# Attention and SiLU MLP on one core: the value products of 39 of 512 key groups as three float16 products of parts

## The chip, the cores and the metric

One core of one Trainium2 chip runs the whole program. The metric is the device time of one execution in microseconds (us); the number to compare is the median of several runs. A difference of under about 0.2% cannot be told from no change here: the three runs of the kernel before lie within 0.66 us of each other.

## The reference

One pre-LayerNorm transformer layer on 2048 tokens of width 512, in float32:

```python
h  = x + softmax((q @ k.T) * 16**-0.5) @ v @ wo      # q, k, v = layernorm(x) @ wqkv; 32 heads of 16
h2 = h + silu(layernorm(h) @ w1) @ w2                # inner width 1792
```

## The kernel before, in words

**Precision.** Most products are of float16 parts: a float32 matrix is split into a high part and the low rest (`low`: rest = matrix - high part), and a product is three products: high by high, low by high, high by low. So it is for the projections, the scores and the MLP. One product stays in float32: the value products, in which the weights of the softmax (`pt`) meet the values (`va`). `PE` here is TensorE, `DVE` VectorE, `ACT` ScalarE, `POOL` GpSimd, `SP` the engine that issues the DMAs.

**Items, groups, steps.** The attention works on 32 items: an item is 4 heads and a block of 512 queries, and items 8b to 8b+7 make block b. An item goes through 16 groups of 128 keys. For a group and a head, `scores` (L495) makes one matrix product of 64 rows into one PSUM bank of kind `st`: 128 keys by 512 queries, where rows 48 and 49 of the operand hold minus the maximum, so that it is subtracted in the product. `weigh` (L504) then has ACT take the exponential of the bank into a tile `pt` of 128 x 512 float32. The scale of that activation comes from a register of ACT (`qk_f`, loaded at L624), and its bias is left at the default. `values` (L893) does the four value products of a group: the 17 columns of `va` of each head (16 and one of ones, which sums the weights) are the weights of TensorE, 128 x 17, in four column groups side by side, and the `pt` of each head streams through; all sum into the bank `pv` over the 16 groups. `finish_item` (L911) copies `pv` out (`pvs`; by DVE in block 0, by ACT later), and sends the sums through DRAM so that POOL can invert them (`invert`, L980), and the result is multiplied by the inverses.

The main loop (L1461) makes one step per group g: maxima for later items, the scores and exponentials of the step, at the end the value products of group g-2 (`LAG = 2`, L1548). `maximum` (L291) finds the maxima that later items need: a product of 48 rows (high parts alone) into one of three banks of kind `sm`, and a `TENSOR_REDUCE` by DVE. Products of 48 or 64 rows take one half of the array's rows, and two of them, in the two halves, run side by side.

**Kinds of steps.** In a *plain* step (block 0's 8 items, and a few steps around the output stages) there are four scores, three maxima, the value products and nothing else; `st` has four banks. Block b's output projection and normalization (`output`, L1291) is put into steps of item 8(b+1). Then, from group 16(8b+9)+4 on, 112 groups carry block b's MLP *beside* them (L485): 56 groups of *first products* (w1), then 56 of *second products* (w2). `beside_products` (L1243) orders such a step: on one half of the array's rows four scores and maxima take turns, on the other six half products of the MLP. One of the four `st` banks then serves the MLP's sum, so that the scores of such a step have three. In a step beside, the scores are of one row half: heads 0 and 2 of groups g and g+1 in an even step, heads 1 and 3 of groups g-1 and g in an odd one. A chain of first products takes 4 steps and ends with `end_first` (L1161): ACT copies the sum out (`g`), two steps later ACT takes a tanh (`t`), and POOL makes the SiLU and its two parts in four instructions (`bend`, L1165). A chain of second products takes 14 steps and ends with `end_second` (L1175): ACT copies the sum (`g`), POOL adds it.

**Order.** Each engine runs its instructions in the order in which the code emits them (`keep_in_program_order`), and waits on semaphores; nothing is reordered by a scheduler. A step is emitted as a whole, so ACT's and POOL's orders follow the steps too.

**Buffers.** `pt` tiles are in two rings, of 6 and 8 (`pt_tile`, L492). Keys and queries of an item lie in a ring of 5 slots (`ks`, `qs`), loaded four items ahead (L256, L261). `zp` has two buffers each for `g` and for the tag `oh` (`t`, `o_t`).

Of the kernel before, what the change touches and what calls it, by code (L numbers as in the profile page):

```python
# [10 lines left out]
F32 = mybir.dt.float32  # L11
F32R = mybir.dt.float32r
F16 = mybir.dt.float16
# [26 lines left out]

BOUND = 23.0
# [8 lines left out]
PTS = 6, 8  # L50

RING = 5

# [14 lines left out]
MORE = (5, 4, 4, 4), (5, 4, 4, 3), (5, 4, 4, 3)  # L68
# [23 lines left out]
def attention_mlp_kernel(ctx: ExitStack, tc: tile.TileContext, x, wqkv, wo, w1, w2, out):  # L92
# [98 lines left out]
    expo = expos[:, :1]  # L191
    minus = const.tile([P, 16], F32, name="minus")
    nc.gpsimd.memset(minus, -1.0)
    ones = const.tile([P, P], F32, name="ones")
    nc.gpsimd.memset(ones, 1.0)
    powers = const.tile([P, 4], F32, name="powers")
    both_s, both_w = powers[:, :2], powers[:, 2:]
    qk_s, qk_w, v_w = (powers[:, n:n + 1] for n in (0, 2, 3))
    qk_e, qk_0, v_f = (const.tile([P, 1], F32, name=name) for name in ("qk_e", "qk_0", "v_f"))
# [3 lines left out]
    w1_s, w2_s, wo_s, o_s = (sigma[:, n:n + 1] for n in range(4))  # L203
# [48 lines left out]

    def rows_of_head(t, h):
        return t[h * DH:(h + 1) * DH].rearrange("d s n -> (d s) n")

    def load_k(i, k, lo=0, n=S):  # L256
        a, j = HEADS[k]
        h = 4 * (i % 8) + 2 * a + j
        dma(ks[i % RING][64 * j:64 * j + 48, a, lo:lo + n], rows_of_head(kd, h)[:, lo:lo + n])

    def load_q(i, k):  # L261
        a, j = HEADS[k]
        h = 4 * (i % 8) + 2 * a + j
        lo = i // 8 * 512
        dma(qs[i % RING][64 * j:64 * j + 48, a, :], rows_of_head(qd, h)[:, lo:lo + 512])
# [25 lines left out]
    def maximum(i, kb, qt, a, j, n):  # L291

        piece = piece_of(i, a)
        width = 1 if i == LAST else 2
        if piece not in mx:
            mx[piece] = small.tile([P, 64], F32, name="mx", bufs=RING + 1)[:, :32 * width].rearrange(
                "p (j a q k) -> p j a q k", j=2, a=width, k=4)
            left[piece] = 32 * width
        heads = (0, 1) if j is None else (j,)
        for m, h in enumerate(heads):  # L300
            mm(space[:, n + m, :], qs[i % RING][64 * h:64 * h + 48, a, qt * P:qt * P + P],
               ks[i % RING][64 * h:64 * h + 48, a, kb * 512:kb * 512 + 512], start=True, stop=True)
# [47 lines left out]
    def place_far(piece):  # L350

        i, a = piece
        n = 16 if a is None else 8
        mt = small.tile([P, P], F16, name="mt", bufs=1)
        pin(nc.sync.dma_start(mt, wide.pop(piece), transpose=True))
        split.pop(piece)

        def out():
            for j in range(2):
                rows = qs[i % RING][64 * j + 48:64 * j + 50, slice(None) if a is None else slice(a, a + 1)]  # L360
                dma(rows.rearrange("r a n -> r (a n)").rearrange("r (a b) -> r a b", b=P), mt[n * j:n * j + n, :])
            placed.add(piece)

        if at["attention"]:
            soon(1, out)
        else:
            out()

    def place_max(piece):

        i, a = piece
        ns = split.pop(piece)
        n = ns.shape[1]
        ps = bank("sm", F16)
        tr(ps[:n, :P], ns, ident_h)
        mt = small.tile([32, P], F16, name="mn", bufs=1)[:n]
        dve("tensor_copy", mt, ps[:n, :P])

        def out():
            for j in range(2):  # L380
                dst = qs[i % RING][64 * j + 48:64 * j + 50, slice(None) if a is None else slice(a, a + 1)]
# [110 lines left out]
    def pt_tile(name, second, dtype=F32):  # L492
        return bp.tile([P, 512], dtype, tag=f"pt{second}", name=name, bufs=PTS[second])

    def scores(g, k, kind="st"):  # L495

        i = g // KC
        a, j, c = head(g, k)
        assert piece_of(i, a) in placed
        ps = bank(kind)  # L500
        mm(ps, ks[i % RING][64 * j:64 * j + 64, a, c * P:(c + 1) * P], qs[i % RING][64 * j:64 * j + 64, a, :],
           start=True, stop=True)
# [40 lines left out]
    rest_sq = const.tile([P, sum(PIECES)], F32, name="rest_sq")  # L543
# [25 lines left out]
    def set_factors():  # L569
# [4 lines left out]
        for to, a, f in ((h_f, inverse[:, :1], 1 / LN), (g_s, w1_s, 1 / 32.0), (g_half, w1_s, 1 / 64.0),  # L574
                         (out_f, inverse[:, :1], 32.0), (o_minus, o_s, -1.0), (o_twice, o_s, 2.0)):
            pool("tensor_scalar", to, a, f, None, op0=ALU.mult)
        pool("tensor_tensor", out_f, out_f, inverse[:, 1:2], ALU.mult)
# [28 lines left out]
    def measure(meanwhile):  # L606
# [13 lines left out]
        dve("reciprocal", v_f, v_w)  # L620
        pool("tensor_scalar", v_f, v_f, 1 / LN, None, op0=ALU.mult)
# [43 lines left out]
    def project_v(b, t):  # L665
# [4 lines left out]
        act("mul", va[:, 4 * b + t, :, 0:DH], ps.rearrange("p (h d) -> p h d", d=DH), v_f)  # L670
# [100 lines left out]
    for b in range(NB):  # L771
# [7 lines left out]
        for n, (kind, k) in enumerate(units + vs if b else units):  # L779
# [160 lines left out]
    def finish_part():  # L940
        pvs = bp.tile([P, 512], F32, name="pvs", bufs=1)
        dve("tensor_copy", pvs, pv)
        o_t = zp.tile([P, 4, P], F32, name="o_t", tag="oh")
# [5 lines left out]
    def divide_part(part, pvs, o_t, kind="st"):  # L949
# [4 lines left out]
        both = gp.tile([P, 4, 2, DH + 1], F32, name="both", bufs=1)  # L954
# [4 lines left out]
        dve("tensor_scalar", rc, rc, o_s, None, op0=ALU.mult)  # L959
# [105 lines left out]
    def load_rows(b, t):  # L1065
        n = 4 * b + t
        if b < NB - 1:
            hx[t] = raw_tile()
        else:
            hx[t] = ks[(LAST + 1) % RING].rearrange("p a n -> p (a n)").bitcast(F32)[:, t * D:(t + 1) * D]  # L1070
# [20 lines left out]
    def gate(ps, engine="dve"):  # L1091
        g, parts = zp.tile([P, 512], F32, name="g"), parts_of(pt_tile("gh", 1))
# [68 lines left out]
    def end_first(f, ps):  # L1161
# [3 lines left out]
        def bend():  # L1165
            t = zp.tile([P, 512], F32, name="t", tag="oh")
# [263 lines left out]
    def maxima(g):  # L1430

        i, c = divmod(g, KC)
        ready = at["ready"] = min(ITEMS, i + RING - (0 if c == KC - 1 else 1)) * 64
# [27 lines left out]
    for g in range(groups):  # L1461
# [11 lines left out]
        if i + RING - 1 < ITEMS and 6 <= c < 14:  # L1473
            (load_k if c % 2 else load_q)(i + RING - 1, c // 2 - 3)
# [30 lines left out]
        if g == 1:  # L1505
            dve("memset", pv, 0.0)
        at["group"] = g
# [76 lines left out]
```

## Time and profile before

| | |
|---|---|
| median of 3 runs | 1549.03 us (1548.48 to 1549.14) |
| the profiled execution | 1548.43 us |
| its span, first to last instruction | 1546.6 us |
| outside the span | 1.8 us |
| PE, DVE, ACT, POOL busy | 99%, 88%, 80%, 37% of the span |
| steps of attention | 180.4 to about 1452 us of the span |

The profile is of one execution. A row that groups instructions has engine, operation, out<-in, shapes and count, then busy time, mean duration of one, and the idle time before them with what ended it. A row of the timeline has the start, how long it took, engine, line, operation and count; equal instructions that follow each other are one row, so the start of a row and the count tell the spacing. `PEld` are weight loads. Ends of matmuls are modelled, so starts are used where a spacing matters. A row of windows has the stretch, its length, then for each engine busy time and count in it.

### The profile page before, as it was taken

What the parts mean: (1) busy time and instruction counts of PE and PEld (TensorE: products, weight loads), DVE (VectorE), ACT (ScalarE), POOL (GpSimd) and SP (SyncE); (2) the same over time, 40 slices, a digit from 0 to 9 for tenths busy, and PEclk for the clock granted to TensorE, in tenths of its full rate; (3) what the DMA queues carried; (4) which work ended last, traced back from release to release, by engine and by line L of the source; (5) the groups of instructions that cost most, each with busy time, mean ns of one, the idle gap of its engine ahead of it and who ended that gap; (6) DMA issues with size and microseconds to landing.
All of it is one profiled execution on the core that took longest, in us unless ns stands there. A gap on an engine that the chain in (4) does not pass through costs nothing.

```text
span 1546.6 us, 30865 instructions
## 1 busy us (share of the span) xinstructions
PE 1536.2 (99%) x11408; PEld 495.2 (32%) x11408; DVE 1365.3 (88%) x2168; ACT 1238.1 (80%) x2410; POOL 576.3 (37%) x782
## 2 busy tenths in 40 slices
PE   9999999999999999999999999999999999999999
PEld 6433322222222333333322333333322333332354
DVE  7899999999999999999999999999999999994322
ACT  5545699999988899888878998888878889888632
POOL 6643454545544444311143444301153444211100
PEclk9999999999999999999999999999999999999999
DMA  6668423433334122344424112444433221335332
GB/s 221 166 173 238 135 81 92 113 100 103 115 84 112 26 63 62 84 145 150 144 64 102 49 45 57 123 134 126 140 78 94 57 61 39 103 101 173 107 90 74
DMA packets 137060, 163.33 MB, mean 106 GB/s; under 512 B 44113, under 2 KB 81041, under 8 KB 136909
## 3 DMA queue, kind: packets, MB, share of 16 engines
q1 hardware_dynamic: 132156, 152.85, 34.8%
q10 hardware_dynamic: 4752, 8.52, 2.1%
q8 instruction: 89, 1.46, 0.4%
q14 instruction: 63, 0.51, 0.1%
HBM read 126.48 MB, written 24.63 MB: 98 GB/s over the span
## 4 chain that ended last, share of the span: by engine, by line
PE 94%; DVE 3%; ACT 2%; issue 1%; POOL 0%; POOLq 0%; ACTq 0%
PE ps L99 93%; DVE mx L305 1%; ACT pt L113 1%; DVE mx L307 1%; PE ps L102 1%; DVE pvs L123 0%; POOL wv_l L106 0%; ACT g L113 0%; ACT pvs L113 0%; DVE ot L123 0%; DVE ks L123 0%; DVE xtl L123 0%; POOL rs L106 0%; ACT wv_h L113 0%; DVE factors L123 0%
## 5 line engine op out<-in xcount | busy, mean ns | idle before, releaser
L307 DVE TENSOR_REDUCE mx<-ps 128x1 f32<-128x512 f32 x1842 | 1147.0, 683 | 59.7 <-PE ps L99 26.3
L113 ACT ACTIVATE pt<-ps 128x512 f32<-128x512 f32 x2048 | 1048.3, 606 | 136.7 <-PE ps L99 134.7
L99 PE MATMUL ps<-ks,qs 48*128 48x512 f16 x2048 | 667.1, 380 | 2.6 <-DVE mx L307 1.5
L99 PE MATMUL ps<-qs,ks 64*128 64x512 f16 x2048 | 629.1, 377 | 0.6
L99 PE MATMUL ps<-pt,va 128*17 128x512 f32 x4096 | 539.1, 598 | 0.6
L99 PE MATMUL ps<-hts,w 64*128 64x512 f16 (+2 forms) x1212 | 285.0, 372 | 0.0
L99 PEld LDWEIGHTS <-ks 64*128 64x128 f16 x2048 | 174.0, 94 | 222.5 <-issue 176.8
L99 PE MATMUL ps<-w,gates 64*128 64x512 f16 (+1 forms) x938 | 230.3, 378 | 0.2 <-ACT g L113 0.2
L99 PEld LDWEIGHTS <-qs 48*128 48x128 f16 x2048 | 166.6, 94 | 68.1 <-issue 28.3
L99 PEld LDWEIGHTS <-w 64*128 64x128 f16 (+1 forms) x1212 | 101.7, 95 | 236.9 <-ACT pt L113 107.2
L106 POOL TENSOR_TENSOR ri<-rc,minus 128x16 f32<-128x16 f32 x31 | 90.7, 2926 | 207.8 <-DMA rc<-dn 207.8
L99 PEld LDWEIGHTS <-gates 64*128 64x128 f16 (+1 forms) x1082 | 88.8, 95 | 222.4 <-ACT pt L113 97.8
L99 PEld LDWEIGHTS ps<-pt,va 128*17 128x17 f32 x4096 | 68.1, 95 | 200.5 <-issue 191.8
L305 DVE TENSOR_REDUCE mx<-ps 128x2 f32<-128x1024 f32 x103 | 119.1, 1219 | 4.3 <-PE ps L99 3.5
L113 ACT ACTIVATE g<-ps,factors 128x512 f32<-128x512 f32 x80 | 55.3, 691 | 65.5 <-PE ps L99 63.9
L106 POOL TENSOR_SCALAR t<-t,factors 128x512 f32<-128x512 f32 x42 | 29.2, 696 | 185.3 <-ACT t L113 185.3
L113 ACT ACTIVATE ks<-ps 128x512 f32<-128x512 f32 x30 | 17.9, 597 | 51.2 <-PE ps L99 45.8
L106 POOL TENSOR_TENSOR ot<-ot,g 128x512 f32<-128x512 f32 x12 | 15.3, 1272 | 115.2 <-ACT g L113 115.2
L123 DVE SCALAR_TENSOR_TENSOR gh<-g,factors,gh 128x512 f16<-128x512 f32 x14 | 10.5, 752 | 52.1 <-ACT gh L113 52.1
L106 POOL TENSOR_TENSOR t<-t,g 128x512 f32<-128x512 f32 x42 | 53.7, 1279 | 3.5
L106 POOL TENSOR_TENSOR sl<-ks,sh 128x512 f16<-128x512 f32 x30 | 34.7, 1158 | 50.4 <-ACT sh L113 34.5
L106 POOL TENSOR_SCALAR nm<-nm 128x16 f32<-128x16 f32 (+1 forms) x42 | 10.8, 258 | 105.3 <-DVE nm L321 103.5
(158 smaller groups left out, 1031.2 us busy)
## 6 DMA issues: line engine op xcount, KB each, us to landing
w<-w2d SPq DMA_DIRECT2D x182, 256.0 KB
ks<-kd SPq DMA_DIRECT2D x120, 192.0 KB
w<-w1d SPq DMA_DIRECT2D x56, 256.0 KB
ks<-in_B_w_dram ACTq DMA_DIRECT2D x28, 256.0 KB
w<-in_B_w_dram SPq DMA_DIRECT2D x28, 256.0 KB
qs<-qd SPq DMA_DIRECT2D x128, 48.0 KB
kd<-sh SPq DMA_DIRECT2D x16, 256.0 KB
qd<-sh SPq DMA_DIRECT2D x16, 256.0 KB
```

Of the source, the lines that this page charges most:

```text
L99: return tc.keep_in_program_order(nc.tensor.matmul(*a, **k))
L102: tc.keep_in_program_order(nc.tensor.transpose(*a))
L106: tc.keep_in_program_order(getattr(nc.gpsimd, op)(*a, **k))
L113: ins = getattr(nc.scalar, fn)(*a, **k)
L123: pin(getattr(nc.vector, fn)(*a, **k))
L305: pin(nc.vector.tensor_reduce(of, space[:, n:n + 2, :], axis=AX.X, op=ALU.max))
L307: pin(nc.vector.tensor_reduce(of[:, j:j + 1], space[:, n, :], axis=AX.X, op=ALU.max))
```

## The change

- In 39 groups (the groups 1, 5, 9 and 13 of an item, where they stand beside second products: 13 in each of the three MLPs) the value products are float16. `scores` then writes the exponential to a float32 tile `raw` and splits it into the two halves of the `pt` tile: the high part by POOL for heads 0 and 1, by ACT for heads 2 and 3, the low part by POOL. `values` does three float16 products of parts for each head, 12 in place of 4. The values of those four chunks are split once, at item 10, by POOL (`split_chunk`).
- So that the parts lie within float16's range, the exponential gets a bias of 14 ln 2 in every group, from a one-column tile `raised`, since sums and values of all groups go into one `pv`. The scale of the values moves into them: POOL multiplies four chunks by `v_s`, and the projection of the values takes a constant factor in place of the tile `v_f`; `o_minus` and `o_twice` are now constants, and two small multiplications of DVE at the end are gone.
- The `pt` tiles are in one ring of 14, in order of use.
- From item 10 on, keys and queries have four ring slots, loaded three items ahead (`slot`, `loaded`); the fifth holds the parts of the values.
- `raw` shares the tag `oh`, now with three buffers; `both`, `ones` and `rest_sq` move to other pools; `mx` has four buffers, before six; one maximum of the output stages moves by some steps (`MORE`).

The diff, cut to its core:

```diff
+RAISE = 14
-PTS = 6, 8
+HALVED = 1, 5, 9, 13
+PTS = 14
 RING = 5
+FEWER = 2 * RING
-MORE = (5, 4, 4, 4), (5, 4, 4, 3), (5, 4, 4, 3)
+MORE = (5, 4, 4, 4), (4, 4, 4, 4), (4, 4, 4, 4)
...
+    raised = const.tile([P, 1], F32, name="raised")
+    nc.gpsimd.memset(raised, RAISE * math.log(2))
...
+    def slot(i):
+        return i % RING if i < FEWER else (i - FEWER) % (RING - 1)
+
+    def loaded(i):
+        return min(ITEMS, i + RING if i < FEWER else max(FEWER + RING - 1, i + RING - 1))
...
-    def pt_tile(name, second, dtype=F32):
-        return bp.tile([P, 512], dtype, tag=f"pt{second}", name=name, bufs=PTS[second])
+    def halves_of(t):
+        return t.bitcast(F16)[:, :512], t.bitcast(F16)[:, 512:]
+
+    width = H * (DH + 1)
+    spare_k, spare_q = (t.rearrange("p a n -> p (a n)") for t in (ks[RING - 1], qs[RING - 1]))
+    parts = [spare_k[:, n * width:(n + 1) * width] for n in range(7)] + [spare_q[:, :width]]
+    split_v = [(parts[n], parts[4 + n]) for n in range(4)]
+
+    def pt_tile(name):
+        return bp.tile([P, 512], F32, tag="pt", name=name, bufs=PTS)
+
+    def in_halves(g):
+        i, c = divmod(g, KC)
+        return FEWER <= i < LAST and c in HALVED and all((x - marks[0]) % (8 * KC) in range(BEHIND + 4 * FC, BEHIND + 8 * FC) for x in (g - 1, g + 3))
+
+    def split_chunk(n):
+        (h, l), v = split_v[n], va[:, HALVED[n]].rearrange("p h d -> p (h d)")
+        pool("tensor_copy", h, v)
+        low(l, v, h, "pool")
...
         def weigh():
-            pts[g, k] = pt_tile("pt", g % 2 if g in beside and not at["alone"] else k // 2)
-            return act("activation", pts[g, k], ps, AF.Exp, scale=qk_f)
+            pts[g, k] = pt_tile("pt")
+            if in_halves(g):
+                raw, (h, l) = zp.tile([P, 512], F32, name="raw", tag="oh", bufs=3), halves_of(pts[g, k])
+                ins = act("activation", raw, ps, AF.Exp, bias=raised, scale=qk_f)
+                if k < 2:
+                    pool("tensor_copy", h, raw)
+                else:
+                    act("copy", h, raw)
+                low(l, raw, h, "pool")
+                return ins
+            return act("activation", pts[g, k], ps, AF.Exp, bias=raised, scale=qk_f)
...
-        act("mul", va[:, 4 * b + t, :, 0:DH], ps.rearrange("p (h d) -> p h d", d=DH), v_f)
+        act("mul", va[:, 4 * b + t, :, 0:DH], ps.rearrange("p (h d) -> p h d", d=DH), 1 / (16.0 * LN))
...
+            if b == 2 and 2 <= n:
+                pool("tensor_scalar", va[:, n - 2, :, 0:DH], va[:, n - 2, :, 0:DH], v_s, 1.0, op0=ALU.mult, op1=ALU.mult)
...
     def values(g):
         i, c = divmod(g, KC)
         n = KC if i < LAST else HALF
+        if in_halves(g):
+            h_l, v_l = [halves_of(pts.pop((g, k))) for k in range(4)], split_v[HALVED.index(c)]
+            for m, (x, v) in enumerate(((0, 0), (0, 1), (1, 0))):
+                for k in range(4):
+                    a, j, keys = head(g, k)
+                    h = 4 * (i % 8) + 2 * a + j
+                    mm(pv[32 * k:32 * k + DH + 1, :], v_l[v][:, (DH + 1) * h:(DH + 1) * (h + 1)], h_l[k][x],
+                       start=False, stop=m == 2 and c == KC - 1)
+            return
...
-        dve("tensor_scalar", rc, rc, o_s, None, op0=ALU.mult)
...
-        if i + RING - 1 < ITEMS and 6 <= c < 14:
-            (load_k if c % 2 else load_q)(i + RING - 1, c // 2 - 3)
+        if loaded(i) > loaded(i - 1) and 6 <= c < 14:
+            (load_k if c % 2 else load_q)(loaded(i) - 1, c // 2 - 3)
...
+        if i == FEWER and c % 3 == 2 and c < 12:
+            split_chunk(c // 3)
```

How the instructions stand now, at the three places of which the prediction speaks. ACT, from the end of the projections (`ks` and `sh` are tiles of these) to the first copy of the first output stage (`g`), that is, all of the first plain stretch of the attention; before:

```order
L113 ACTIVATE ks_106<-ps 128x512
L113 CAST sh<-ks_106 128x512
L113 ACTIVATE pt<-ps 128x512 x544
L113 ACTIVATE g<-ps,factors 128x512
L113 ACTIVATE pt<-ps 128x512 x4
```

And now:

```order
L121 ACTIVATE ks_105<-ps 128x512
L121 CAST sh<-ks_105 128x512
L121 ACTIVATE pt<-ps,raised 128x512 x544
L121 ACTIVATE g<-ps,factors 128x512
L121 ACTIVATE pt<-ps,raised 128x512 x4
```

The order and the counts are the same; each exponential reads one more operand, the column `raised`, as the copy `g` reads a column of `factors`. So it is with all 2048 exponentials.

ACT at the end of the first MLP's first products and the start of its second products (`g` the copy of a chain's sum, `t` its tanh, `pvs` the copy of an item's result); before:

```order
L113 ACTIVATE g<-ps,factors 128x512
L113 ACTIVATE pt<-ps 128x512 x6
L113 ACTIVATE t<-g 128x512
L113 ACTIVATE pt<-ps 128x512 x20
L113 COPY pvs<-ps 128x512
L113 ACTIVATE pt<-ps 128x512 x30
```

And now:

```order
L121 ACTIVATE g<-ps,factors 128x512
L121 ACTIVATE pt<-ps,raised 128x512 x4
L121 ACTIVATE raw<-ps,raised 128x512 x2
L121 CAST pt<-raw 128x512
L121 ACTIVATE t<-g 128x512
L121 ACTIVATE pt<-ps,raised 128x512 x2
L121 ACTIVATE raw<-ps,raised 128x512 x2
L121 CAST pt<-raw 128x512
L121 ACTIVATE pt<-ps,raised 128x512 x10
L121 ACTIVATE raw<-ps,raised 128x512 x2
L121 CAST pt<-raw 128x512
```

In two steps out of four the last exponential of the step is followed by a cast that reads it, and `t` stands behind such a cast.

POOL at the same place (`nm` and `ns` belong to an item's maxima; `t`, `gates` are the four instructions of `bend`); before:

```order
L106 CAST ns_110<-nm 128x2x8
L106 TENSOR_TENSOR ns_110<-nm,ns_110 128x2x8
L106 TENSOR_SCALAR t<-t,factors 128x512
L106 TENSOR_TENSOR t<-t,g 128x512
L106 CAST gates<-t 128x512
L106 TENSOR_TENSOR gates<-t,gates 128x512
```

And now:

```order
L114 CAST ns_109<-nm 128x2x8
L114 TENSOR_TENSOR ns_109<-nm,ns_109 128x2x8
L114 CAST pt<-raw 128x512
L114 TENSOR_TENSOR pt<-raw,pt 128x512 x2
L114 TENSOR_SCALAR t<-t,factors 128x512
L114 TENSOR_TENSOR t<-t,g 128x512
L114 CAST gates<-t 128x512
L114 TENSOR_TENSOR gates<-t,gates 128x512
L114 CAST pt<-raw 128x512
L114 TENSOR_TENSOR pt<-raw,pt 128x512 x2
```

The last `bend` of the first products now stands between the splitting of the first and of the second pair of heads of the first split group.

PE's order is otherwise that of before: the same scores, maxima and MLP products stand between the value products of each group, but for one maximum in each of the last two output stages that moves by three steps; in 39 groups 12 products of 17 columns stand in place of 4.

More of the change, by code (lines that the diff above doesn't have):

```diff
@@ L359, in out @@
             for j in range(2):
-                rows = qs[i % RING][64 * j + 48:64 * j + 50, slice(None) if a is None else slice(a, a + 1)]
+                rows = qs[slot(i)][64 * j + 48:64 * j + 50, slice(None) if a is None else slice(a, a + 1)]
                 dma(rows.rearrange("r a n -> r (a n)").rearrange("r (a b) -> r a b", b=P), mt[n * j:n * j + n, :])
@@ L541, in attention_mlp_kernel @@
     sq = small.tile([P, 3], F32, name="sq", bufs=1)
-    rest_sq = const.tile([P, sum(PIECES)], F32, name="rest_sq")
+    rest_sq = wp.tile([P, sum(PIECES)], F32, name="rest_sq")
+    ones = wp.tile([P, P], F32, name="ones")
+    nc.gpsimd.memset(ones, 1.0)
     norms = const.tile([P, 4], F32, name="norms")
@@ L942, in finish_part @@
         dve("tensor_copy", pvs, pv)
-        o_t = zp.tile([P, 4, P], F32, name="o_t", tag="oh")
+        o_t = zp.tile([P, 4, P], F32, name="o_t", tag="oh", bufs=3)
         pool("memset", o_t, 0.0)
@@ L1091, in gate @@
     def gate(ps, engine="dve"):
-        g, parts = zp.tile([P, 512], F32, name="g"), parts_of(pt_tile("gh", 1))
+        g, parts = zp.tile([P, 512], F32, name="g"), parts_of(pt_tile("gh"))
         act("activation", g, ps, AF.Silu, scale=h_f)
@@ L1165, in bend @@
         def bend():
-            t = zp.tile([P, 512], F32, name="t", tag="oh")
+            t = zp.tile([P, 512], F32, name="t", tag="oh", bufs=3)
             act("activation", t, z, AF.Tanh, scale=0.5)
```

34 lines of the change are left out of this document (16 added, 18 removed).

## The prediction

> **What bounds the kernel now.** I read the page first, then the stretches of the attention as windows, then single steps in the timeline.
>
> ```profile
> PE 1536.2 (99%) x11408; PEld 495.2 (32%) x11408; DVE 1365.3 (88%) x2168; ACT 1238.1 (80%) x2410; POOL 576.3 (37%) x782
> L113 ACT ACTIVATE pt<-ps 128x512 f32<-128x512 f32 x2048 | 1048.3, 606 | 136.7 <-PE ps L99 134.7
> ```
>
> PE is busy all the time, and ACT waits for PE before its 2048 exponentials, so by the page PE sets the time and ACT has 20% to spare. The windows say how this share is spread: the plain steps of block 0, then first products, second products, and the last second products.
>
> ```profile
> 180.41:436.32 255.91, 254.12 (x1920) 56.18 (x1920) 244.75 (x392) 252.96 (x515) 123.63 (x184) 1.00 0.38 107
> 497.50:644.31 146.81, 146.81 (x1234) 47.40 (x1232) 139.63 (x229) 131.71 (x256) 68.72 (x82) 1.00 0.24 64
> 644.31:781.40 137.09, 137.09 (x1147) 44.01 (x1145) 129.56 (x213) 111.25 (x216) 19.64 (x27) 1.00 0.43 130
> 1328.90:1403.52 74.62, 74.62 (x623) 23.75 (x621) 70.01 (x116) 60.21 (x118) 12.59 (x17) 1.00 0.38 116
> ```
>
> The fourth number after the length is ACT. In plain steps it is busy for 252.96 of 255.91 us: no share to spare, beside a PE that is as full. Grouped by line and form for that whole run of plain steps, to its end at 451.57, ACT shows
>
> ```profile
> L113 ACT ACTIVATE pt<-ps 128x512 f32<-128x512 f32 x544 | 268.2, 612 | 3.0 <-PE ps L99 3.0
> ```
>
> These are the 544 exponentials that the order has in one row: 268.2 + 3.0 = 271.2 us, 0.50 us each (1.99 a step), with 3.0 us of waiting in all.
>
> Two steps of second products in the timeline, with the value products, two MLP products, the exponentials and the fourth score:
>
> ```profile
> 720.65 1.05 PE L99 MATMUL ps<-pt,va 128*17 128x512 f32 x8
> ...
> 721.64 0.39 PE L99 MATMUL ps<-w,gates 64*128 64x512 f16 x1
> ...
> 722.08 0.38 PE L99 MATMUL ps<-w,gates 64*128 64x512 f16 x1
> ...
> 722.35 2.07 ACT L113 ACTIVATE pt<-ps 128x512 f32<-128x512 f32 x4 [0.60 <-PE ps L99]
> ...
> 723.00 0.37 PE L99 MATMUL ps<-qs,ks 64*128 64x512 f16 x1
> 723.30 0.13 PEld L99 LDWEIGHTS ps<-pt,va 128*17 128x17 f32 x8 [0.37 <-issue]
> 723.30 1.05 PE L99 MATMUL ps<-pt,va 128*17 128x512 f32 x8
> ...
> 724.94 2.07 ACT L113 ACTIVATE pt<-ps 128x512 f32<-128x512 f32 x4 [0.52 <-PE ps L99]
> ...
> 725.61 0.37 PE L99 MATMUL ps<-qs,ks 64*128 64x512 f16 x1
> ...
> 725.92 1.05 PE L99 MATMUL ps<-pt,va 128*17 128x512 f32 x8
> ```
>
> Call the first MLP product of a step T. The value products take 0.99 (720.65 to 721.64, the first T), so the second T is 723.30 + 0.99 = 724.29. In the second step the first exponential starts 0.65 after T, the fourth score at T+1.32, the value products 0.31 later, and the step takes 2.62 (723.30 to 725.92). In the first step the first exponential starts 0.71 after T and, at 0.60 each, ends at 722.95; the fourth score starts at 723.00, T+1.36, and the step takes 2.65. There are three score banks, so the fourth score needs the bank of the first exponential: it starts at T+1.32 or 0.05 after the end of that exponential, whichever is later. This is a loop through PE and ACT (first exponential, fourth score, value products, first score of the next step) with little to spare: 0.65 + 0.60 + 0.05 = 1.30 against 1.32.
>
> **The change part by part.** *PE, removed.* A stream of 512 columns in float16 takes 0.22 (two from 721.64 to 722.08). The float32 value products take 0.99, four such streams and about 0.11; three take one less, 0.77. 39 groups by 0.21 is 8.3 us off, if PE still sets the time; the loop above keeps the gain, since the value products lie in it.
>
> *ACT, the bias.* Every exponential now reads a column. No exponential or other activation of the trace has a column as its bias; the nearest rows have one as the scale, and differ in nothing else:
>
> ```profile
> L113 ACT ACTIVATE va<-ps,v_f x12: 687/688/691, 37.8 to 90.6; 128x512 f32<-128x512 f32 x12
> L113 ACT ACTIVATE va<-ps x4: 595/598/602, 16.3 to 20.7; 128x512 f32<-128x512 f32 x4
> ...
> 581.41 0.69 ACT L113 ACTIVATE g<-ps,factors 128x512 f32<-128x512 f32 x1
> 581.98 3.11 ACT L113 ACTIVATE pt<-ps 128x512 f32<-128x512 f32 x6
> 584.95 0.65 ACT L113 ACTIVATE t<-g 128x512 f32<-128x512 f32 x1
> 585.64 2.06 ACT L113 ACTIVATE pt<-ps 128x512 f32<-128x512 f32 x4
> ```
>
> A column costs 688 - 598 = 90 ns, and it isn't hidden behind the next instruction: after `g`, with a column, the next begins 0.57 later; exponentials follow each other at (2.06 - 0.60)/3 = 0.49. So I take 0.57 for an exponential and 0.69 until its end. Ends: nothing (the bias is read in passing) to the whole 0.09; I take the whole, the nearest row.
>
> The Trainium skill says the same of the bias itself (ScalarE: Activation LUTs, "What ACT_TABLE_LOAD costs"): an ACTIVATE with immediate scale and bias takes 186 ns + 0.833 ns per element, and each column operand adds about 93 ns. The trace agrees for a scale (90 ns); for a bias no run so far shows it.
>
> Plain steps: 544 by 0.57 is 310.1 where 271.2 stood: **+39**. PE, which now fills a step of 1.99, will wait for ACT's four exponentials, 2.28. About 20 more plain steps lie around the three output stages, 0.3 each: **+6**.
>
> First products, 56 steps in each block: the first exponential ends at T+0.65+0.69 = 1.34, the fourth score comes at 1.39 instead of 1.32, a step takes 2.68. 56 by 2.68 is 150.0 against 146.8 (the window): +3.2. In such a step the loop needs 2.68 and ACT 4 by 0.57 = 2.28, so ACT has 0.40 to spare. The copy `g` (0.57) in one step of four overruns that by 0.17, the tanh (0.69, 584.95 to 585.64) by 0.29; the next first exponential is late by that and the loop can't catch up: 14 by 0.17 and 13 by 0.29, +6.2. Three blocks: **+28**. The lower end is nothing: 224 exponentials by 0.57, 14 by 0.57, 13 by 0.69 and three item copies by 0.5 make about 146, just the stretch's length, if ACT never waited.
>
> *ACT, the casts.* A cast that reads what the instruction before it wrote, among the projections:
>
> ```profile
> 131.00 0.60 ACT L113 ACTIVATE ks<-ps 128x512 f32<-128x512 f32 x1 [1.70 <-PE ps L99]
> 131.63 0.62 ACT L113 CAST sh<-ks 128x512 f16<-128x512 f32 x1
> 132.15 0.62 ACT L113 ACTIVATE ks<-ks 128x512 f32<-128x512 f32 x1
> ```
>
> The cast starts 0.63 after the activation, 0.03 past its end; the next instruction follows 0.52 later. With the column, a step with a cast takes ACT 3 by 0.57, then 0.72, then 0.52: 2.95, more than the loop's 2.68. Of four steps two have casts (2.95 each), one is plain (2.68) and one has the shorter value products (2.46): 11.05 against 2 by 2.61 and 2 by 2.65, 10.52. So 0.53 per split group although PE's gain is in it; 13 groups, +6.9 a block. Then what meets a step with a cast and pushes the next one back in full: the item copy, of the same size as a cast, 0.52, behind the cast of group 1, three times; `g` of two chains, 0.57 each; the tanh between the first two casts, 0.69; two more `g` in shorter steps and the last plain steps, about 0.5: +3.9.
>
> *POOL.* The last two rows of a `bend` are the split that it now makes for two of the heads (a copy of 0.61, a subtraction of 1.16; for the others 1.16 alone):
>
> ```profile
> 638.14 0.69 POOL L106 TENSOR_SCALAR t<-t,factors 128x512 f32<-128x512 f32 x1 [1.78 <-ACT t L113]
> 638.91 1.28 POOL L106 TENSOR_TENSOR t<-t,g 128x512 f32<-128x512 f32 x1
> 640.26 0.61 POOL L106 CAST gates<-t 128x512 f16<-128x512 f32 x1
> 640.95 1.16 POOL L106 TENSOR_TENSOR gates<-t,gates 128x512 f16<-128x512 f32 x1
> ```
>
> That is 5.9 us in four steps of 11 us; the values need the parts three steps after their first exponential, about 9.5 us, and they are done after about 8.5. Only the first group of a block has a `bend` (638.14 to 640.95 + 1.16 = 642.11, 4.0) in the middle, as the order shows: there I take a wait of 1 us (0 to 2). Two blocks of +11.8 and the third's 9 groups, +8: **+32**.
>
> What I cost at nothing: DVE's maxima (129.56 busy of 137.09 in the second products; none is added, and the steps get longer). The keys come one item later, still a whole item ahead of their first maximum; were they late, each would cost the rest of its transfer once. POOL's four multiplications of `va` fall into projections that wait for nothing of POOL. The single ring of 14 frees a tile before it is asked for, and takes a second semaphore wait from the first exponential of odd steps (its 0.71 instead of 0.65), which the column's 0.09 covers.
>
> Sum: 39 + 6 + 28 + 32 = +105. The profiled execution takes 1548.4 (0.6 below the median): **1653 us**.
>
> **The rivals.** *The bias is free* (0.08). Then PE's 8.3 come off, and about 3 more for the second waits; the casts just fit (3 by 0.49 + 0.63 + 0.52 = 2.62), but the copies, `g` and the tanh behind them push back as above, about 9, and POOL about 5: 1551, no change that can be told. For it: no row shows a bias column. Against it: the rows of the scale.
>
> *Faster* (0.06). The bias is free, and the things behind the casts are hidden, as a late ACT only costs PE beyond the banks: 1548.4 - 8.3 - 3 = 1537. It decides at the fourth score after an item copy: if it still comes at T+1.32. Against it speaks the 0.05 after the first exponential's end.
>
> *PE's issue is slower than its streams* (0.05). 1234 matmuls and 1232 loads in 146.81 us are 60 ns each; if that were the sequencer's limit, the 24 instructions of a split group would take 1.43 and not 0.77, 39 by 0.66 = 26 more: 1679. Against it: the eight loads at 723.30 pass within 0.13 us, so they had been fetched ahead. The Trainium skill has such a limit (TensorE: Matmul & The Clock Gate, "Wait — 56ns, not 53.3ns?"): with hardware decode off the sequencer spends about 62 ns on a MATMUL, otherwise start to start never falls under about 25 ns. The 0.13 for eight loads speaks for the second; the first would make the 1679.
>
> *The lags of ACT are caught up* (0.10): the loop has slack that I don't see. Then only the plain steps, the casts and half of the rest are lost: 39 + 6 + 14 + 20, about 1627.
>
> **How the numbers follow.** The forecast has 0.71 (with a spread of some 15 us: 0.57 for an exponential may be 0.56 to 0.59, 10 us in the plain steps alone). From 1620 to 1682 it takes in the caught-up lags and the slow issue and leaves out the free bias. Faster by over 0.2% (about what can be told from no change) only where the bias is free: 0.06; within 0.2%: 0.07; slower: 0.87.
>
> **What would show it.** Right: exponentials of about 698 ns; plain steps of 2.28; ACT busy nearly all of block 0, with PE waiting for `pt`; first products in about 156 us, second ones in about 149; 17-column products of 0.77 in 39 groups. Wrong: exponentials of 606 ns, and with them everything but the 8.3.

## The result, and the profile after

| | before | after |
|---|---|---|
| median | 1548.78 us (4 runs, 1548.48 to 1549.14) | 1660.82 us (4 runs, 1660.45 to 1660.94) |
| ratio | | 1.0722, 95% interval [1.0708, 1.0737] |
| span of the profiled execution | 1546.6 us | 1659.1 us |

The changed kernel is 112 us slower; the forecast was 1653, in a range from 1620 to 1682. Lines of the kernel have moved: L113 is now L121, L99 is L107, L106 is L114.

Engine shares from the page, and the group of the exponentials that write `raw`:

```profile
PE 1608.4 (97%) x11548; PEld 501.0 (30%) x11548; DVE 1365.2 (82%) x2165; ACT 1442.5 (87%) x2480; POOL 785.3 (47%) x1004
L121 ACT ACTIVATE raw<-ps,raised 128x512 f32<-128x512 f32 x140 | 88.8, 695 | 0.8 <-POOL pt L114 0.5
```

An exponential takes 695 ns in place of 606. There are 140 of these: 35 split groups by four heads. The text ahead of the prediction and its term for PE say 39, 13 in each block; that was miscounted. The third block has 9, as the prediction's term for POOL has it.

The run of plain exponentials (the same 544 as before), grouped by line and form:

```profile
L121 ACT ACTIVATE pt<-ps,raised 128x512 f32<-128x512 f32 x544 | 314.4, 1073 | 0.0
```

Where it took 271.2 us with 3.0 us of waiting, it takes 314.4 with none. The mean of 1073 ns is no longer the time of one: the records of a full ACT overlap, each a little longer than the one before (up to 1137 ns), and only the sum over the count, 0.578, is a spacing.

Windows over the same groups as before (plain steps of block 0, first products, second products, last second products):

```profile
180.95:477.21 296.26, 273.79 (x1920) 58.73 (x1919) 245.82 (x392) 296.26 (x515) 123.24 (x184) 1.00 0.33 93
542.01:698.29 156.28, 155.76 (x1233) 47.34 (x1232) 139.55 (x229) 150.11 (x258) 79.84 (x95) 1.00 0.21 55
698.29:847.07 148.78, 145.01 (x1197) 45.24 (x1197) 129.46 (x213) 141.77 (x240) 90.14 (x101) 1.00 0.41 118
1431.87:1514.00 82.13, 79.11 (x649) 24.55 (x648) 70.07 (x116) 77.47 (x132) 54.29 (x61) 1.00 0.35 106
```

In plain steps ACT is busy for the whole 296.26 us; PE's 273.79 for the same 1920 products, 254.12 before, hold some of its waits. The first products take 156.28 (156 was forecast), the second ones 148.78 (149), though ACT is not full in either: 150.11 and 141.77. There it is the loop that sets the time. One step of second products and the split value products that end it, in the timeline:

```profile
709.33 0.39 PE L107 MATMUL ps<-w,gates 64*128 64x512 f16 x1
...
709.98 3.81 ACT L121 ACTIVATE pt<-ps,raised 128x512 f32<-128x512 f32 x6 [0.25 <-PE ps L107]
...
710.71 0.37 PE L107 MATMUL ps<-qs,ks 64*128 64x512 f16 x1
...
711.02 0.82 PE L107 MATMUL ps<-pt,ks 128*17 128x512 f16 x12
711.87 0.09 PEld L107 LDWEIGHTS <-gates 64*128 64x128 f16 x1 [0.53 <-ACT pt L121]
...
711.87 0.39 PE L107 MATMUL ps<-w,gates 64*128 64x512 f16 x1
```

T is 709.33. The first exponential starts at T+0.65, takes 0.69, and the fourth score follows at T+1.38 (1.39 was forecast). The split value products start 0.31 after it, but the next step begins 0.85 later and not 0.77: the third exponential, at 709.98 + 2 by 0.57 = 711.12, ends at 711.81, and the load for the next step's first MLP product, at 711.87, waits for ACT. The wait is an order that both kernels prescribe (`fence`, with `after`): the first half product of a step must follow the first exponential that was emitted behind the last half product of the step before, which here is the third. That is a second loop through PE and ACT, which the prediction had not seen; it takes 0.65 + 1.14 + 0.69 + 0.06 = 2.54 a step, so a split group's shorter step stops there and not at 2.46.

ACT at a step with a cast, and at one with the item's copy behind the cast:

```profile
746.61 1.26 ACT L121 ACTIVATE pt<-ps,raised 128x512 f32<-128x512 f32 x2 [0.15 <-PE ps L107]
747.76 1.26 ACT L121 ACTIVATE raw<-ps,raised 128x512 f32<-128x512 f32 x2
749.06 0.62 ACT L121 CAST pt<-raw 128x512 f16<-128x512 f32 x1
749.58 1.26 ACT L121 ACTIVATE pt<-ps,raised 128x512 f32<-128x512 f32 x2
750.73 1.26 ACT L121 ACTIVATE raw<-ps,raised 128x512 f32<-128x512 f32 x2
752.03 0.62 ACT L121 CAST pt<-raw 128x512 f16<-128x512 f32 x1
752.55 0.58 ACT L121 COPY pvs<-ps 128x512 f32<-128x512 f32 x1
753.03 2.43 ACT L121 ACTIVATE pt<-ps,raised 128x512 f32<-128x512 f32 x4
```

From 746.61 to 749.58 is 2.97 (2.95 was forecast), and ACT doesn't wait in it; the copy adds 753.03 - 752.55 = 0.48 to the next.

### The profile page after: what moved, and what is told of

Its sections match the earlier page's. It is cut to its first block, busy times and chain, and to the rows that moved or that the text cites. A ratio compares the mean times of both kernels' runs of the same rounds, so it can differ in the third digit from the quotient of the medians.

```text
span 1659.1 us, 31346 instructions
## 1 busy us (share of the span) xinstructions
PE 1608.4 (97%) x11548; PEld 501.0 (30%) x11548; DVE 1365.2 (82%) x2165; ACT 1442.5 (87%) x2480; POOL 785.3 (47%) x1004
## 4 chain that ended last, share of the span: by engine, by line
PE 66%; ACT 27%; POOL 2%; DVE 2%; issue 1%; DMA 1%; SPq 0%; ACTq 0%; POOLq 0%
PE ps L107 65%; ACT pt L121 25%; ACT raw L121 1%; POOL pt L114 1%; DVE mx L320 1%; ACT g L121 1%; ACT pvs L121 0%; PE ps L110 0%; DMA va<-in_A_wqkv_dram 0%; POOL t L114 0%; DMA ks<-in_A_x_dram 0%; POOL gates L114 0%; DVE st L131 0%; SPq L137 0%; DVE xtl L131 0%
## 5 line engine op out<-in xcount | busy, mean ns | idle before, releaser
L121 ACT ACTIVATE pt<-ps,raised 128x512 f32<-128x512 f32 x1908 | 1144.1, 815 | 45.4 <-PE ps L107 42.0
L107 PE MATMUL ps<-qs,ks 64*128 64x512 f16 x2048 | 684.6, 377 | 36.1 <-ACT pt L121 34.8
L107 PE MATMUL ps<-ks,qs 48*128 48x512 f16 x2048 | 669.1, 380 | 1.3 <-DVE mx L320 0.9
L107 PE MATMUL ps<-pt,va 128*17 128x512 f32 x3816 | 502.8, 598 | 0.4
L107 PE MATMUL ps<-hts,w 64*128 64x512 f16 (+2 forms) x1212 | 285.0, 372 | 0.0
L107 PEld LDWEIGHTS <-ks 64*128 64x128 f16 (+1 forms) x2424 | 182.6, 93 | 225.6 <-issue 192.3
L107 PE MATMUL ps<-w,gates 64*128 64x512 f16 (+1 forms) x938 | 230.3, 378 | 2.2 <-ACT g L121 0.8
L107 PEld LDWEIGHTS <-qs 48*128 48x128 f16 x2092 | 167.2, 94 | 89.6 <-issue 35.8
L107 PEld LDWEIGHTS <-w 64*128 64x128 f16 (+1 forms) x1212 | 101.7, 95 | 237.1 <-ACT pt L121 107.2
L114 POOL TENSOR_TENSOR pt<-raw,pt 128x512 f16<-128x512 f32 x140 | 159.6, 1161 | 5.6
L107 PEld LDWEIGHTS <-gates 64*128 64x128 f16 (+1 forms) x1082 | 89.0, 95 | 217.6 <-ACT raw L121 54.0
L107 PEld LDWEIGHTS ps<-pt,va 128*17 128x17 f32 x3816 | 63.3, 95 | 286.3 <-issue 274.6
L114 POOL TENSOR_TENSOR ri<-rc,minus 128x16 f32<-128x16 f32 x31 | 90.6, 2923 | 117.2 <-DMA rc<-dn 117.2
L114 POOL TENSOR_SCALAR t<-t,factors 128x512 f32<-128x512 f32 x42 | 29.0, 691 | 200.7 <-ACT t L121 200.7
L121 ACT ACTIVATE g<-ps,factors 128x512 f32<-128x512 f32 x80 | 55.1, 689 | 61.3 <-PE ps L107 60.0
L121 ACT ACTIVATE raw<-ps,raised 128x512 f32<-128x512 f32 x140 | 88.8, 695 | 0.8 <-POOL pt L114 0.5
L114 POOL CAST pt<-raw 128x512 f16<-128x512 f32 x70 | 42.6, 609 | 97.0 <-ACT raw L121 96.8
L121 ACT ACTIVATE ks<-ps 128x512 f32<-128x512 f32 x30 | 17.9, 597 | 49.5 <-PE ps L107 43.6
L114 POOL TENSOR_TENSOR sl<-ks,sh 128x512 f16<-128x512 f32 x30 | 34.7, 1156 | 50.1 <-ACT sh L121 31.9
L114 POOL TENSOR_TENSOR t<-t,g 128x512 f32<-128x512 f32 x42 | 53.6, 1276 | 3.5
```

What stands on the lines that cost most here:

```text
L107: return tc.keep_in_program_order(nc.tensor.matmul(*a, **k))
L114: tc.keep_in_program_order(getattr(nc.gpsimd, op)(*a, **k))
L121: ins = getattr(nc.scalar, fn)(*a, **k)
```

## The experiments

Two edits of the change can be taken away alone: the column (a bias of 14 ln 2 may also stand in the instruction as a number, with the same value), and the split groups. The first four runs make a table of both, with the kernel before and a column beside it.

| median, us | column | number or none |
|---|---|---|
| kernel before | 1642.7 | 1548.8 |
| change without split groups | 1635.8 | 1544.1 |
| change with 35 split groups | 1660.8 | 1553.2 |

**The column alone, in the kernel before.**

```diff
+    raised = const.tile([P, 1], F32, name="raised")
+    nc.gpsimd.memset(raised, 0.0)
...
-            return act("activation", pts[g, k], ps, AF.Exp, scale=qk_f)
+            return act("activation", pts[g, k], ps, AF.Exp, bias=raised, scale=qk_f)
```

> The kernel before, whose exponentials get a bias column of zeros and nothing else. Theory (the column costs 0.09 us on each exponential, and ACT's loop passes it on): the profile of the changed kernel shows +43 us over the 544 plain exponentials and about +25 over the first products; the second products without casts are 56 steps of 2.68 instead of 2.63, with g and tanh about +4 a block; some +5 for plain steps around the output stages; and the second semaphore wait, which this kernel still has in a quarter to a half of the steps, is no longer covered but added, about +7: 1549 + 43 + 25 + 12 + 5 + 7 = 1641, and at least 1625. An exponential takes about 695 ns. Rival (the splitting of the weights on ACT and POOL makes the loss, a column is read in passing): 1549 within 5, exponentials of 606 ns.

Measured: 1642.69 us, ratio 1.0606 [1.0588, 1.0624]. Its windows for the plain steps and the first products:

```profile
180.55:476.81 296.26, 273.86 (x1921) 58.81 (x1920) 245.87 (x392) 296.26 (x515) 123.20 (x184) 1.00 0.34 93
541.61:697.82 156.21, 156.21 (x1234) 47.46 (x1233) 139.85 (x229) 148.94 (x256) 68.49 (x82) 1.00 0.23 60
```

The same 296.26 as in the changed kernel: in the plain steps the whole loss is this one operand of the exponential, here a column of zeros. That the first products agree too (156.21 and 156.28) is in part chance. The changed kernel without split groups, a run further down, takes less for the same groups:

```profile
542.57:697.98 155.41, 155.41 (x1234) 47.35 (x1233) 139.60 (x229) 149.12 (x256) 75.84 (x90) 1.00 0.20 54
```

So the change saves 0.8 there by its other edits, and its first casts, which fall into the last four steps of that window, cost 0.9. The theory stands, with its number; the rival, near 1549, falls.

**The changed kernel with the number in place of the column.**

```diff
-                ins = act("activation", raw, ps, AF.Exp, bias=raised, scale=qk_f)
+                ins = act("activation", raw, ps, AF.Exp, bias=RAISE * math.log(2), scale=qk_f)
...
-            return act("activation", pts[g, k], ps, AF.Exp, bias=raised, scale=qk_f)
+            return act("activation", pts[g, k], ps, AF.Exp, bias=RAISE * math.log(2), scale=qk_f)
```

> The changed kernel with the bias 14 ln 2 as an immediate number instead of the column; the same values. Theory: exponentials of 606 ns again, plain steps of 1.96 to 1.99; what is left is PE's gain, 35 groups by the measured 0.13 = -4.5, the second waits that one ring takes away, -4, what meets a cast on ACT, +9, and the wait for POOL in the first split group of each block, +4: about 1553 (1545 to 1560). Rival (the splits cost by themselves what they cost in the changed kernel, +32 by the sum): 1575 or more. Second rival (the column was not the cause at all): 1655 or more.

Measured: 1553.20 us, ratio 1.0027 [1.0017, 1.0038]. Its windows of plain steps and of the second products:

```profile
180.57:436.54 255.97, 254.18 (x1921) 56.23 (x1920) 244.70 (x392) 253.02 (x515) 123.25 (x184) 1.00 0.38 107
644.54:782.58 138.04, 136.16 (x1199) 45.14 (x1197) 128.68 (x212) 123.74 (x240) 90.07 (x101) 1.00 0.44 128
```

The plain steps are back at the 255.91 of before. The second products, 137.09 before, stay at 138.04: PE's busy time has fallen, yet the stretch has not. ACT and PE at the same place as above, where the item's copy stands behind a cast, and at the split value products that follow:

```profile
651.26 1.09 ACT L121 ACTIVATE raw<-ps 128x512 f32<-128x512 f32 x2
652.38 0.62 ACT L121 CAST pt<-raw 128x512 f16<-128x512 f32 x1
652.91 0.58 ACT L121 COPY pvs<-ps 128x512 f32<-128x512 f32 x1
653.38 2.06 ACT L121 ACTIVATE pt<-ps 128x512 f32<-128x512 f32 x4
```

```profile
653.33 0.38 PE L107 MATMUL ps<-qs,ks 64*128 64x512 f16 x1
654.04 0.37 PE L107 MATMUL ps<-qs,ks 64*128 64x512 f16 x1
...
656.95 0.83 PE L107 MATMUL ps<-pt,ks 128*17 128x512 f16 x12
...
657.71 0.39 PE L107 MATMUL ps<-w,gates 64*128 64x512 f16 x1
```

The first exponential of the step comes at 653.38, ends at 653.38 + 0.60 = 653.98, and the fourth score at 654.04 is late with it. Without a column the split value products take 657.71 - 656.95 = 0.76, the 0.77 of the prediction: the second loop, 0.65 + 2 by 0.49 + 0.60 + 0.06 = 2.29, is short enough again. So a split group brings 0.23, and each of the copies and chains' sums behind a cast costs 0.49 or 0.56.

**The changed kernel without split groups, with the column.**

```diff
-        return FEWER <= i < LAST and c in HALVED and all(...)
+        return False and all(...)
```

> The changed kernel with no group split: all value products in float32, the column still read by every exponential, one ring of score tiles, four ring slots of keys. Theory: the changed kernel's 1660.8 less what its split groups add over plain second products with the column: about 0.53 + 0.08 for each of 35 groups, 21, the waits for POOL 3 to 4, what meets a cast 9: about 1627 (1620 to 1635). Rival (the rings and slots, not the column, make the loss): it makes no difference to this run, which then stays near 1627 too, and the next run tells.

Measured: 1635.77 us, ratio 1.0561 [1.0543, 1.0578]. 9 us more than the theory's 1627, and just outside its range: the split groups add 25.0 with the column, not the nearly 34 of the theory. Its 0.53 + 0.08 for a group was too much: the 0.53 was counted from steps of 2.61 and 2.65, but with the column these take 2.67, so that four steps of a split group, 11.16 against 10.69, add 0.47. And part of what meets a cast (`g`, the tanh, the copy) costs something without a cast too. The run lies 6.9 under the kernel before with a column. In the profiles every fourth step of the first products and every second one of the second products has fallen from 2.74 to 2.67; that fits the single ring, which takes the second wait from the first exponential of such steps, but the ring was not tried alone.

**Neither column nor split groups.** Both edits above together.

> The changed kernel with no group split and the bias as an immediate number: what is left of the change is the one ring of score tiles, the four slots of keys, the moved maximum and the smaller edits. Theory: they cost nothing, and the single ring takes the second semaphore wait from the first exponential of odd steps, 0.037 in about 116 steps: 1549 - 4 = 1545 (1543 to 1549). Rival (the rings and slots cost time by themselves): over 1552.

Measured: 1544.13 us, ratio 0.9970 [0.9958, 0.9981], 4.6 us faster than before. The rings and slots cost nothing that shows, and the gain is the one that was said of the single ring: the same steps as above fall from 2.65 to 2.61. Split groups cost 1553.2 - 1544.1 = 9.1 without the column and 25.0 with it; so of the 112 us 91.6 are the column alone (93.9 in the kernel before), -4.6 the ring and the smaller edits, 9.1 the splits, and 16.0 come only where column and splits meet.

**All copies of high parts by POOL** (with the number as bias).

```diff
-                if k < 2:
-                    pool("tensor_copy", h, raw)
-                else:
-                    act("copy", h, raw)
+                pool("tensor_copy", h, raw)
```

> The run with the immediate bias, with the high parts of all four heads copied by POOL, so that ACT has no cast. Theory (what is left of the splits' price is what stands behind a cast on ACT: the item's copy, g, the tanh, about 0.5 us each time, and POOL's bend in the first group): the steps of 3.10 and 3.17 fall to 2.61 where POOL is in time; POOL now takes about 7.3 us for a group, and the parts are needed 7.4 us after the first exponential, so it is just in time, and late by about 1 us where an addition of g or a maximum comes between, three or four times a block: 1553 - 9 + 9, about 1553 (1547 to 1558), with the price moved from ACT to POOL. Rival (the casts on ACT are the whole price): 1542 to 1546.

Measured: 1566.29 us, ratio 1.0114 [1.0099, 1.0130]: over both. ACT's collisions are gone, as the theory has it, but POOL is later than it had said. POOL and PE at the first split group of block 1:

```profile
643.34 1.15 POOL L114 TENSOR_TENSOR gates<-t,gates 128x512 f16<-128x512 f32 x1
644.44 0.61 POOL L114 CAST pt<-raw 128x512 f16<-128x512 f32 x1
645.13 1.15 POOL L114 TENSOR_TENSOR pt<-raw,pt 128x512 f16<-128x512 f32 x1
646.23 0.61 POOL L114 CAST pt<-raw 128x512 f16<-128x512 f32 x1
646.92 1.16 POOL L114 TENSOR_TENSOR pt<-raw,pt 128x512 f16<-128x512 f32 x1
```

```profile
646.89 0.38 PE L107 MATMUL ps<-pt,ks 128*17 128x512 f16 x1 [1.40 <-POOL pt L114]
...
648.13 0.38 PE L107 MATMUL ps<-pt,ks 128*17 128x512 f16 x1 [0.63 <-POOL pt L114]
```

PE waits for the last high part (646.23 + 0.61), then for the last low part (646.92 + 1.16). And in a later group the score of the next item waits for its maxima, which come by DMA:

```profile
692.14 0.37 PE L107 MATMUL ps<-qs,ks 64*128 64x512 f16 x1 [1.66 <-DMA qs<-mt]
```

That second way had not been priced. POOL had the parts of the maxima ready at 681.3. SP issues in order: at 680.54 it issued the store of `ot`, just after POOL had ended the addition for it, which stood behind splits (679.25 + 1.26 = 680.51), and the loads that followed kept SP until 684.29, when it issued the maxima's transposition. Why their way into `qs` was issued only at 689.6 stays open. Step by step against the run without split groups, the first group of each block costs 2.8, and the three waits for this DMA 1.8, 2.7 and 1.0. The price of a split was moved from ACT to POOL and grew.

**Without the first split group of each block** (number as bias).

```diff
-        return FEWER <= i < LAST and c in HALVED and all(...)
+        return FEWER <= i < LAST and c in HALVED and all(...) and g not in (205, 333, 461)
```

> The run with the immediate bias, without the first split group of each block (three of 35), where POOL's last bend of the first products and ACT's last tanh stand between the casts. Theory: each block loses the wait of 1.47 in that group and the 0.49 and 0.04 of ACT three steps before: 3 by 2.0 = 6: 1547 (1546 to 1549). Rival (POOL is late in the next group instead, or the wait had another cause): 1551 or more.

Measured: 1547.88 us, ratio 0.9993 [0.9984, 1.0002], as the theory has it: three groups of 35 had cost 5 us.

**13 chosen groups** (number as bias).

```diff
-        return FEWER <= i < LAST and c in HALVED and all(...)
+        return g in (213, 221, 229, 237, 253, 341, 349, 357, 365, 381, 469, 477, 485)
```

> The run with the immediate bias, with 13 split groups instead of 35: those whose casts meet no item's copy, no g and no tanh on ACT, no bend on POOL and no end of a maximum on DVE. Theory: ten of them keep 0.227, three half of it, and nothing is paid for them: 1544.1 (no split) - 2.6 = 1541.5 (1541 to 1543). Rival (splits cost what they bring, wherever they stand): 1544 or more.

Measured: 1542.46 us, ratio 0.9959 [0.9945, 0.9973]; 1.7 under the run without splits where 2.6 was expected. In the profile all 13 steps are shorter, ten by 0.227 and three by 0.112, and no step of the second products is longer. What is missing is one wait in the last item, for weights of the MLP (that step is 0.87 longer). By the times alone the 1.7 could hardly be told from no change, being 0.11%; it rests on the steps of the profile:

```profile
PE ps L107 <- DMA w<-w2d: 0.7, 1, 0.7
```

**21 groups, copies by POOL in 17 of them** (number as bias; a list of groups as above).

> The immediate bias and 21 split groups: each is one where the run with all copies on POOL, or for four of them the run with casts on ACT, showed its gain of 0.227 without a wait. POOL copies the high parts of all heads in 17 groups, ACT those of two heads in four. Theory (a split pays only where ACT and POOL have no other work near): 18 or 19 by 0.227 and two by 0.11 off the run without splits, 1544.1 - 4.4 = 1539.7 (1539 to 1542; a late transfer of weights, as the run with 13 groups has one of 0.88, may come on top). Rival (splits cost what they bring): 1544 or more.

Measured: 1542.16 us, ratio 0.9953 [0.9939, 0.9966], not told apart from the run with 13 groups. In the profiled execution (1543.2) 18 of the 21 steps bring what was expected, 3.9 in all, but new waits take 3.4 back. The largest is at a group with ACT's casts, where POOL first sat waiting for an item's inverses:

```profile
1060.12 1.27 POOL L114 TENSOR_TENSOR ot<-ot,den 128x512 f32<-128x512 f32 x1 [8.47 <-DMA den<-dr]
1061.36 0.27 POOL L114 TENSOR_SCALAR nm<-nm 128x16 f32<-128x16 f32 x1
1061.69 0.20 POOL L114 CAST ns<-nm 128x16 f16<-128x16 f32 x1
1061.97 0.22 POOL L114 TENSOR_TENSOR ns<-nm,ns 128x16 f16<-128x16 f32 x1
1062.13 0.61 POOL L114 CAST pt<-raw 128x512 f16<-128x512 f32 x1
```

The maxima and the parts stood behind that wait; the step there took 4.13 in place of 2.61. Whether POOL's changed order brought this wait there or a late transfer in this one execution stays open.

**A second column** (the changed kernel without split groups, its scale from a column too).

```diff
-            return act("activation", pts[g, k], ps, AF.Exp, bias=raised, scale=qk_f)
+            return act("activation", pts[g, k], ps, AF.Exp, bias=raised, scale=qk_e)
```

> The changed kernel with no split group, with the exponential's scale read from a column too in place of the register. Theory (each column costs ACT 0.09 on each exponential, plain steps pass on all four, steps beside other work pass on the one that stands in the loop first exponential, fourth score, value products, and ACT's whole work where g or the tanh adds to it): against the run without splits, plain steps 2.31 + 0.37 = 2.68, 136 + 17 steps by 0.37 = 57; first products 2.675 + 0.09 = 2.77, steps with g 2.68 + 0.67 = 3.35 and with the tanh somewhat less, some 16 a block, 48; second products 54 by 0.09 and g and copies on top, 7 a block, 20: 1635.8 + 57 + 48 + 20 = about 1760 (1735 to 1775). Exponentials of about 790 ns. Rival (only the first column costs, a second is read beside it): 1636 within 3.

Measured: 1770.72 us, ratio 1.1433 [1.1415, 1.1450]; the rival falls. Its windows of plain steps and first products:

```profile
181.51:524.28 342.77, 293.41 (x1921) 63.08 (x1920) 246.37 (x393) 342.77 (x515) 123.20 (x184) 1.00 0.29 80
594.20:764.49 170.29, 163.58 (x1234) 46.21 (x1233) 139.92 (x229) 169.28 (x256) 75.71 (x90) 1.00 0.19 49
```

A plain step takes 342.77 / 128 = 2.68, as expected. The run with one column has 296.55 for the same 128 groups, so the second column costs (342.77 - 296.55) / 512 = 0.090 an exponential. A step of first products without other work takes 2.82, not the 2.77 that the first loop gives: the second loop, by the third exponential, is 0.65 + 2 by 0.67 + 0.79 + 0.06 = 2.84.

## Why the prediction was right, step by step

- **The column costs an exponential 0.09, and it isn't hidden.** Shown: 695 against 606 ns, the same 296.26 us with the column alone, and 255.97 with the number in its place. The copies of `va`, which lose their column in the change, go the other way, from 688 to 597 ns. In a full ACT the spacing grows by 0.085, from 268.2 / 544 = 0.493 to 0.578. The Trainium skill's figure (ScalarE: Activation LUTs, "What ACT_TABLE_LOAD costs"), about 93 ns for each column operand, agrees with the measured 89 for a bias and 90 for a scale.
- **Plain steps +39.** The stretch of 544 went from 271.2 to 314.4, +43.2: 46.2 more work for ACT, less the 3.0 of waiting that is gone. The term was small by 4, since the spacing in a full ACT is 0.578, not the 0.57 taken from one row behind `g`. **Plain steps around the output stages +6**: with 1 at the first stage, 2.5 at each of the others, the steps between the marks of the same groups give 6.0.
- **First products +28.** 156.28 - 146.81 = 9.47 a block, 28.4. The loop (first exponential, fourth score, value products) gives 2.675 a step against 2.68. `g` cost 0.22 (0.17) and the tanh 0.16 (0.29), about 1 us a block less than was taken. That the window agrees to 0.1 us is in part luck: its last four steps already belong to the second products, and the 0.9 of the first casts, which the prediction had counted there, makes up for it.
- **Second products +32.** 148.78 - 137.09 = 11.7 (11.8 with POOL's 1 us) and 82.13 - 74.62 = 7.5 in the last block; with the steps between and behind these windows that the other terms do not count, 34. Steps with a cast, 2.97 (2.95). The wait for POOL in a block's first group, whose products take 1.90 and not 0.85, is 1.05 (1 was taken); its row stands below.
- **PE's 8.3 off.** Wrong in both factors: 35 groups, and 0.13 each, 4.5 in all. The 0.77 for three streams was right, as the run with the number shows; what failed was "the loop above keeps the gain, since the value products lie in it": another loop, by the third exponential and the order laid on the next MLP product, ends 0.08 to 0.09 later once the exponentials are slow. In the second products' term the shorter step was taken as 2.46; it is 2.54 to 2.55.
- **The single ring at nothing.** Its gain was said to be covered by the column's 0.09. It is not covered: with the column it is about 6.9 us (if those are the ring's), without it 4.6. The forecast had it in all the same, since its steps of 2.68 start from the 0.65 of a step without the second wait.
- **The free bias** was the rival for no change, at 1551. With the number in place of the column, its case in fact, the kernel takes 1553.2: its price for copies, `g` and tanh behind casts holds. **Slow issue of PE** falls as it was priced: 24 instructions in 0.76 are 32 ns each, not 60. A limit on the 12 products alone, 63 ns each there, would not show in this row. **Lags caught up** falls: the first products lose 9.5, and 8.6 in the run without split groups, where half was said.
- **The sum**: 43.2 + 6 + 28.4 + 34 and 0.5 ahead of the attention (180.95 against 180.41) make 112, where 105 was forecast; most of the difference is the plain steps' 4 and the second products' 2.

The wait for POOL in the first group, the last of its 12 products:

```profile
699.89 0.38 PE L107 MATMUL ps<-pt,ks 128*17 128x512 f16 x1 [0.72 <-POOL pt L114]
```

## What to carry to other kernels

Before an operand is added to the instruction that an engine repeats most, price it by a row with and without such an operand and multiply by the count in stretches where that engine is full, not by its mean share: ACT's 80% over the span hid a stretch at 99%. A constant belongs into the instruction and not into a column, where the language takes it as a number. And work moved from the bound engine to one with room pays only where that engine's own queue has room at the moment: here 13 chosen groups beat 35.

## What the runs showed that was not expected

- Two loops hold a step beside other work, and which binds depends on the exponential's duration: with 0.60 the first (fourth score), with 0.69 the second (third exponential, then the next step's first MLP product) where the value products are short, with 0.79 the second also where they are long (2.82 a step).
- Among the 35 groups of the run with the number, seven of chunk 9 (217, 233 and 249 in block 1, and so in the others: 345, 361, 377, 473) have the short value products and yet a step of 2.61 or 2.62. In that step DVE has an item's last reduction ahead of its maxima; here at group 217:

```profile
677.39 1.87 DVE L320 TENSOR_REDUCE mx<-ps 128x1 f32<-128x512 f32 x3
679.37 0.22 DVE L334 TENSOR_REDUCE nm<-mx 128x16 f32<-128x64 f32 x1
679.51 1.88 DVE L320 TENSOR_REDUCE mx<-ps 128x1 f32<-128x512 f32 x3
```

  PE's last maximum of that step comes 0.64 after the one before, 0.42 in the step of group 209. So DVE takes the gain where it is as full as PE; no run moved that reduction to show it.
